# Two ways of loading q and k for the last eight attention units of a fused attention and two-MLP kernel

## The chip, the cores and the metric

The kernel runs as one program on one core of a Trainium2 chip. The metric is the device time of one execution in microseconds. Each kernel is run several times and the median stands for it. One further execution is run under the hardware profiler, and every row of a trace in this document is from such a profiled execution.

## The reference, cut to what matters

q, k and v are float32 arrays of 8 batches x 8 heads x 576 rows x 64 columns. Attention is computed within chunks of 64 rows only:

```
scores = (q_c @ k_c^T) / 8          # per batch, head and chunk of 64 rows
attn   = softmax(scores)            # minus the row's maximum, exp, divided by the row's sum
x      = attn @ v_c                 # laid out as 4608 tokens x 512
xn     = x / rms(x) * rms_g
x      = (silu(xn @ w_gate) * (xn @ w_val)) @ w_out          # 512 -> 1536 -> 512
out    = (h * relu6(h + 3) / 6) @ w_out2 ,  h = x @ w_in2    # 512 -> 2048 -> 512
```

## The kernel before

TensorE's time goes to the two MLPs. Their weights and activations are each split into a high and a low part, and three products of 128x128 by 128x512 (high x high, low x high, high x low) stand for one. The 4608 tokens are nine blocks of 512. The first three blocks run through the first MLP one by one (36 steps each), with the weights in SBUF. The other six run in three **passes** of two blocks, in which seven sums of operands replace eight products. Operands of the passes are read again from device memory, 512 KB at a time, by `Loads.ahead` (line 472 for the operands of the up products, `wo`, and line 478 for those of the down products, `wd`). Six such transfers are issued ahead, and each use of one issues another, so that a `wo` is asked for six operands before its use. An operand serves 12 products.

**The clock of the order.** The program's order is written out by hand in steps called ticks. `tick()` (line 1199) first emits what the agenda holds for this tick and then calls `some(n)` (line 1145), which takes n waiting transfers from a queue of attention loads and issues them on SP (SyncE's queue). n is 3 in the passes. A pass has 66 ticks: 42 of the up products, with 12 products (one operand) in each, and 24 of the down products, with 12 products in each. P0 is the first tick of the passes. All engines run their own instructions in this order, and SP issues its transfers in this order too.

**Attention** is worked in units of 256 tokens and is spread between the products. Units 4 to 9 (class `Pair`, line 737) run under the first three blocks, units 10 to 17 (class `Wide`, line 891, a subclass of `Pair`) under the first two passes, four to a pass, at ticks 0, 14, 28 and 42 of the pass. `STEPS_P` (line 43) lists their steps: turn_q at 0, turn_k at 1, then scores, maximum, subtraction, exp, sum, and so on until values at 13. `attend` (line 1162) runs a step. When it has run turn_k of a unit it hands q and k of the next unit to the queue (`give`), and when it has run values it hands over v. Before turn_q it calls `until`, which issues at once whatever of this unit's q and k is still in the queue.

- `Pair.parts_qk` (line 751) places heads so that 64 rows of SBUF hold one head's 64 columns after a turn. It reads runs of 32 columns (128 bytes): one transfer moves 32 rows x 8 runs, 32 KB, and a unit needs 16 transfers each for q and k (24 each where it crosses the end of a batch with 64 and 192 tokens, 32 each where it crosses with 128 and 128).
- `Wide.parts_qk` (line 894) reads eight rows of a head at once (2 KB) for two heads. One transfer moves 128 KB, and a unit needs 4 each for q and k (8 each where it crosses a batch).
- `turned` is a transpose of 32x32 blocks on VectorE. In `Pair` it reads and writes in plain order (line 780), in `Wide` with strides (line 908).
- `Pair.scores` (line 790) multiplies over 64 rows and makes all scores of the unit in 32 products of 64x64 by 64x64. `Wide.scores(e)` (line 913) multiplies over 32 rows and sums two such products, so that 32 products make half of the unit's scores, e = 0 or 1. It runs twice, at ticks 3 and 5 of the unit, with its own maximum (`top`, line 936) behind each. A float32 product shows as two instructions in the trace, so that 32 products are 64 instructions.

The buffers of q, k, their turned forms and v are single: the first transfer into q waits until the unit before has turned its q, and likewise for k. The passes also carry `Stash` (line 281), which prepares the second MLP's weights on VectorE, ScalarE and GpSimd and loads and stores them on ScalarE's own queue: 16 transfers in 24 ticks.

Of the kernel before, what the change touches and what calls it, by code (L numbers as in the profile page):

```python
# [10 lines left out]
F32 = mybir.dt.float32  # L11
# [3 lines left out]
ALU = mybir.AluOpType  # L15
AX = mybir.AxisListType


def _f32_of(word):
# [23 lines left out]
STEPS_P = (  # L43
    (0, ("turn_q",)),
    (1, ("turn_k",)),
    (3, ("scores0", "top0")),
    (5, ("scores1", "top1")),
    (6, ("less",)),
    (7, ("expo",)),
    (9, ("total", "share")),  # L50
# [24 lines left out]
def fused_kernel(  # L75
# [13 lines left out]
    nc = tc.nc  # L89
    B, H, S, D = q.shape  # L90
    NT, DM = out.shape
    CH = 64
# [6 lines left out]
    NP = H // 2  # L99
# [14 lines left out]
    sm_p = ctx.enter_context(tc.tile_pool(name="sm", bufs=4))  # L114
# [10 lines left out]
    PS = ps_p.tile([128, 8, 512], F32, name="PS")  # L125
    yd = [dr_p.tile([128, KD, N], F32, name=f"yd{b}") for b in range(NB)]
    ATT, GB, VB, YB = 0, 2, 3, 4
# [358 lines left out]
    def runs(t0, n):  # L486
        done = 0
        while done < n:
            b, s = divmod(t0 + done, S)
            step = min(n - done, S - s)  # L490
            yield done, step, b, s
            done += step
# [5 lines left out]
    def side(a, j):  # L498
        return j ^ a // 2

    class Att:
# [37 lines left out]
        def scores(self):  # L539
            self.s = PS[:, self.bank:self.bank + 2, 0:256]  # L540
            ps = self.s.rearrange("p z (e c k) -> p z e c k", e=2, c=2)
            qT = self.qT.rearrange("p (a t) -> p a t", a=NP)
            kT = self.kT.rearrange("p (a t) -> p a t", a=NP)
            for a, c, j in FOURS:
                x = side(a, j)
                nc.tensor.matmul(
                    ps[x * 64:(x + 1) * 64, a // 2, a % 2, c, :],
                    qT[j * 64:(j + 1) * 64, a, c * 64:(c + 1) * 64],
                    kT[j * 64:(j + 1) * 64, a, c * 64:(c + 1) * 64],
                    start=True,  # L550
                    stop=True,
                )

        def top(self):
            self.mx = sm_p.tile([128, 2, NP], F32, tag="mx", name="mx")
            s = self.s.rearrange("p z (x k) -> p z x k", k=CH)
            nc.vector.tensor_reduce(out=self.mx, in_=s, axis=AX.X, op=ALU.max)
# [111 lines left out]
        def run(self, *steps):  # L669
            for st in steps:  # L670
                getattr(self, st)()

    class Half(Att):
# [12 lines left out]
        def parts_qk(self):  # L686
            self.q, self.k = self.bufs("q", "k")
            for dst, src in ((self.q, q), (self.k, k)):
                d = dst.rearrange("p (h d) -> p h d", h=H)
                for off, n, b, s in runs(self.i * 128, 128):  # L690
                    nc.sync.dma_start(out=d[off:off + n], in_=src[b, :, s:s + n, :].rearrange("h p d -> p h d"))
                    yield
# [41 lines left out]
    TP = 256  # L734
    NPR = NT // TP

    class Pair:
# [38 lines left out]
                    nc.sync.dma_start(out=d[off:off + n], in_=v[b, :, s:s + n, :].rearrange("h p d -> p h d"))  # L776
                    yield

        def turned(self, to, x):
            nc.vector.transpose(out=to, in_=x)  # L780

        def turn_q(self):
            self.qT = self.buf("qT")
            self.turned(self.qT, self.q)

        def turn_k(self):
            self.kT = self.buf("kT")
            self.turned(self.kT, self.k)

        def scores(self):  # L790
            ps = PS[:, ATT:ATT + 2, :].rearrange("p z (t e c k) -> p z t e c k", t=2, e=2, c=2)
# [90 lines left out]
            nc.vector.tensor_tensor(ss, sq[:, 0:256], sq[:, 256:512], op=ALU.add)  # L882

        def run(self, st):
            if st[-1].isdigit():
                getattr(self, st[:-1])(int(st[-1]))
            else:
                getattr(self, st)()


    class Wide(Pair):


        def parts_qk(self):

            self.q, self.k = self.buf("q"), self.buf("k")
            for dst, src in ((self.q, q), (self.k, k)):
                d = dst.rearrange("p (h x) -> p h x", h=2)
                for off, n, b, s in runs(self.i * TP, TP):
                    for g in range(4):  # L900
                        h = g // 2 + 2 * (g % 2)
                        sv = src[b, h:h + 5:4, s:s + n, :].rearrange("h (t u) d -> t h (u d)", u=8)
                        r = g * 32 + off // 8
                        nc.sync.dma_start(out=d[r:r + n // 8], in_=sv)
                        yield

        def turned(self, to, x):
            nc.vector.transpose(
                out=to.rearrange("p (h g t u) -> p h u g t", h=2, g=2, u=8),
                in_=x.rearrange("p (h u g f) -> p h u g f", h=2, u=8, g=2),  # L910
            )

        def scores(self, e):
            ps = PS[:, ATT:ATT + 2, :].rearrange("p z (t e c k) -> p z t e c k", t=2, e=2, c=2)
            self.s = PS[:, ATT:ATT + 2, :].rearrange("p z (x k) -> p z x k", k=CH)
            qT, kT = (
                x.rearrange("p (h g n) -> p g h n", h=2, g=2) for x in (self.qT, self.kT)
            )
            for t in range(2):
                for y in range(2):  # L920
                    for g in range(2):
                        for h in range(2):
                            for j in range(2):
                                c = h ^ y
                                f = slice((2 * j + e) * 32, (2 * j + e + 1) * 32)
                                n = slice((2 * t + c) * 64, (2 * t + c + 1) * 64)
                                x = side(2 * h + e, j)
                                nc.tensor.matmul(
                                    ps[x * 64:(x + 1) * 64, h, t, e, c, :],
                                    qT[f, g, h, n],  # L930
                                    kT[f, g, h, n],
                                    start=g == 0,
                                    stop=g == 1,
                                )

        def top(self, e):
            if e == 0:
                self.mx = sm_p.tile([128, 2, 2 * NP], F32, tag="mx", name="mx")
            nc.vector.tensor_reduce(
                out=self.mx.rearrange("p z (t e c) -> p z t e c", t=2, e=2)[:, :, :, e],  # L940
                in_=self.s.rearrange("p z (t e c) k -> p z t e c k", t=2, e=2)[:, :, :, e],
                axis=AX.X,
                op=ALU.max,
            )

    XN = {}

# [168 lines left out]
    with tc.manual_schedule():  # L1116
# [20 lines left out]
                first[int(op[-1])].run(op[:-1])  # L1137
        xf.pop(0)

        unit = [(Pair if i < 10 else Wide)(i) for i in range(NPR)]  # L1140
        chain = [Half(i) for i in range(NTL, 2 * NTL)] + unit[4:]
        supply = deque()
        ready = set()
# [1 line left out]
        def some(n):  # L1145

            while n > 0 and supply:
                if next(supply[0][1], True):
                    ready.add(supply.popleft()[0])
                else:  # L1150
                    n -= 1
# [44 lines left out]
        P0 = 2 * HK  # L1196
        clock = [-HK]

        def tick():
            t = clock[0]  # L1200
            for _, fn in sorted(agenda.pop(t, ()), key=lambda x: x[0]):
                fn()
            some(8 if t < 0 else 5 if t < P0 - 14 else 3)
            clock[0] += 1

        for blk, due in (
# [118 lines left out]
        for b in range(3):  # L1325
            prev, late = None, None
            hk = 0
            for f in range(FA):
                mm_up(GB, whole(W["gate", f]), xs)
                s = sg_p.tile([128, N], F32, tag="sg", name="sg")  # L1330
# [33 lines left out]
        for p in range(3):  # L1364
            b = 3 + 2 * p
            bk = {0: (2, 3), 1: (6, 7), 4: (4, 5)} if p % 2 == 0 else {0: (6, 7), 1: (2, 3), 4: (4, 5)}
            g = {}
# [16 lines left out]
            for i in range(NI + 1):  # L1384
# [13 lines left out]
                for n, (pr, m) in enumerate(slots):  # L1398
                    i_ = i - 1 if pr in (3, 4) else i
                    k_, x, z = {  # L1400
                        1: (S00, B11, 0), 2: (S01, B21, 0), 3: (S4, B22, 4), 4: (S11, T4, 1),
                        5: (S1, T1, 4), 6: (S2, T2, 1), 7: (S3, T3, 1),
                    }[pr]
# [14 lines left out]
                    elif (pr, m) == (3, 0):  # L1418
                        t = gt(h0, 1)
                        vec(t, t, bank(4, 0), ALU.add)  # L1420
                        later = t
                    elif (pr, m) == (4, 1):
                        t = gt(h1, 0)
# [3 lines left out]
                    elif (pr, m) == (3, 1):  # L1427
                        s = hold.pop("s2")
                        vec(s, s, bank(4, 1), ALU.add)
                        t = gt(h0, 1)  # L1430
# [8 lines left out]
                    elif (pr, m) == (2, 1):  # L1439
                        t = gt(f0, 0)  # L1440
                        vec(t, t, bank(0, 1), ALU.mult)
                    elif (pr, m) == (7, 0):
                        t = gt(f1, 1)
# [3 lines left out]
                    elif (pr, m) == (7, 1):  # L1447
# [3 lines left out]
                        t = gt(f1, 1)  # L1451
                        nc.gpsimd.tensor_tensor(t, t, s3, op=ALU.mult)
                    if n % 2 == 1:
                        tick()
# [67 lines left out]
        for n, f in enumerate(fs):  # L1522
            bank = 6 + n % 2
            i, m, z = f // 4, f // 2 % 2, f % 2
# [5 lines left out]
            s = sg_p.tile([128, N], F32, tag="sg", name="sg")  # L1530
# [124 lines left out]
        for b in range(1, NB, 2):  # L1655
# [7 lines left out]
            for I in range(NG + 1):  # L1663
# [7 lines left out]
                for pr, m in slots:  # L1671
                    I_ = I - 1 if pr in (3, 4) else I
                    i = 2 * I_ + m
                    k_, x, z = {
                        1: (A11, B11, Z0), 2: (A12, B21, Z0), 3: (S4_, B22, Z4), 4: (A22, T4, Z1),
                        5: (S1_, T1, Z4), 6: (S2_, T2, Z1), 7: (S3_, T3, Z1),
                    }[pr]
# [14 lines left out]
                    elif pr == 3:  # L1692
                        t = slot(i, "12")
# [7 lines left out]
                    elif pr == 7:  # L1701
                        t = slot(i, "22")
# [37 lines left out]
            for n, (pr, i) in enumerate(steps):  # L1740
                k_, z = {
                    1: (O11, Z0), 2: (O12, Z0), 3: (O4, Z4), 4: (O22, Z1),
                    5: (O1, Z4), 6: (O2, Z1), 7: (O3, Z1),
                }[pr]
# [7 lines left out]
                if i == NQ - 1:  # L1752
# [5 lines left out]
                    elif pr == 7:  # L1758
                        c = keep("c22", Z1)
# [4 lines left out]
                    elif pr == 3:  # L1764
                        c = held.pop("u2")
# [15 lines left out]
        for m in range(2):  # L1781
            for i in range(NQ):
                for wi, xi in ((0, 0), (1, 0), (0, 1)):
# [4 lines left out]
                        start=False,  # L1788
                        stop=False,
# [37 lines left out]
```

## Time and profile before

| | us |
|---|---|
| median of 3 runs | 1682.11 (1678.25 to 1682.73) |
| the profiled execution, whole | 1679.51 |
| its span, first to last instruction | 1677.7 |

The profile's views show, for one execution, the share of each engine, groups of instructions by line of the kernel, who waited for whom, and instructions in order of time. PE is TensorE's products and PEld its weight loads, DVE is VectorE, ACT is ScalarE, POOL is GpSimd, SPq and ACTq are the queues on which SyncE and ScalarE issue transfers. Times of rows are us from the span's start. The passes begin at about 379 us.

### The profile page before, as it was taken

To read this page: it belongs to the slowest core of one execution; us is meant where nothing else is said; L and a number is where in the kernel's file an instruction comes from. 1 tells how busy PE (TensorE), PEld (TensorE's weight loads), DVE (VectorE), ACT (ScalarE), POOL (GpSimd) and SP (SyncE) were. 2 spreads that over 40 slices of the span, in tenths; PEclk is the share of its full clock that TensorE was granted. 3 is DMA by queue.
4 is the path that set the end of the run, shared out by engine and by line. 5 is a ranking of instruction groups with operands and counts; after the bars stand their busy time and mean duration, and the time that the engine had idled before them with its cause. 6 is when DMAs were issued, how large, how long until landed. Compare 5 with 4: busy or idle time off the path is not lost.

```text
span 1677.7 us, 26541 instructions
## 1 busy us (share of the span) xinstructions
PE 1649.2 (98%) x9920; PEld 1350.7 (81%) x9920; DVE 1086.8 (65%) x1600; ACT 845.2 (50%) x1409; POOL 459.5 (27%) x336
## 2 busy tenths in 40 slices
PE   8999999999999999999999999999999999999998
PEld 7777888878878888788887888888788878887886
DVE  6998566656575775758436378448746764874475
ACT  6786344455454454645434344455445544654552
POOL 1001434321326522364226622131023003301310
PEclk8999999999999999999999999999999999999999
DMA  9913777747876488855979766667767786777665
GB/s 301 271 37 71 207 208 222 205 152 251 292 262 224 168 297 286 290 176 185 361 238 316 293 239 226 213 190 250 219 209 224 209 243 191 223 218 235 189 200 150
DMA packets 336096, 375.07 MB, mean 224 GB/s; under 512 B 184288, under 2 KB 260064, under 8 KB 335840
## 3 DMA queue, kind: packets, MB, share of 16 engines
q1 hardware_dynamic: 273984, 302.84, 58.4%
q10 hardware_dynamic: 61984, 70.53, 12.2%
q8 instruction: 79, 1.29, 0.3%
q14 instruction: 49, 0.40, 0.1%
HBM read 292.55 MB, written 80.74 MB: 223 GB/s over the span
## 4 chain that ended last, share of the span: by engine, by line
PE 45%; DVE 5%; DMA 1%; ACT 1%; issue 1%; SPq 1%; DVEq 0%; POOL 0%; ACTq 0%; POOLq 0%
PE PS L1034 24%; PE PS L1584 13%; PE PS L1023 2%; DVE gs L1578 1%; PE PS L1051 1%; PE PS L1048 1%; PE PS L1049 1%; DVE gt L1720 1%; PE PS L1056 1%; PE PS L1057 1%; PE PS L1060 1%; SPq L1603 1%; DMA stash_in<-sc 1%; PE PS L1784 1%; DVE oq L1598 0%
## 5 line engine op out<-in xcount | busy, mean ns | idle before, releaser
L1034 PE MATMUL PS<-xu,wo 128*128 128x512 f32 x1512 | 353.1, 392 | 3.4 <-DVE gu L1362 2.3
L1034 PEld LDWEIGHTS PS<-xu,wo 128*128 128x128 f32 x1512 | 282.3, 188 | 65.0 <-DVE gu L1362 3.1
L1034 PE MATMUL PS<-xo,wq 128*128 128x512 f32 x1344 | 305.3, 389 | 0.0
L1584 PE MATMUL PS<-gs,wq 128*128 128x512 f32 x1296 | 296.2, 390 | 2.4 <-DVE gs L1578 2.0
L1034 PEld LDWEIGHTS PS<-xo,wq 128*128 128x128 f32 x1344 | 252.3, 188 | 52.4
L1584 PEld LDWEIGHTS PS<-gs,wq 128*128 128x128 f32 x1296 | 242.7, 188 | 55.3 <-DVE gs L1578 5.0
L1023 PE MATMUL PS<-XH,w 128*128 128x512 f32 x576 | 148.9, 401 | 5.1 <-ACT sg L1331 3.1
L1023 PEld LDWEIGHTS PS<-XH,w 128*128 128x128 f32 x576 | 108.0, 191 | 29.2 <-ACT sg L1331 3.8
L1048 PE MATMUL PS<-gs,wd 128*128 128x512 f32 x288 | 113.4, 394 | 1.6 <-DVE gu L1362 1.6
L1049 PE MATMUL PS<-gs,wd 128*128 128x512 f32 x288 | 112.2, 390 | 0.0
L1079 POOL TENSOR_TENSOR al<-sg,ah 128x512 fp32r<-128x512 f32 x40 | 56.2, 1404 | 156.2 <-ACT ah L1077 151.9
L1358 POOL TENSOR_TENSOR gs<-gu,gs 128x512 fp32r<-128x512 f32 x60 | 86.6, 1461 | 42.7 <-ACT gs L1357 33.9
L1651 POOL TENSOR_TENSOR gt<-gx 128x512 f32<-128x512 f32 x8 | 10.3, 1289 | 299.8 <-DVE gx L1648 299.8
L1362 DVE TENSOR_TENSOR gu<-gu,PS 128x512 f32<-128x512 f32 x60 | 41.0, 685 | 77.4 <-ACT gu L1444 42.0
L1578 DVE TENSOR_TENSOR gs<-gu,gs 128x512 fp32r<-128x512 f32 x88 | 67.9, 792 | 31.4 <-ACT gs L1577 31.1
L1577 ACT CAST gs<-gt 128x512 fp32r<-128x512 f32 x96 | 58.3, 623 | 49.6 <-DVE gt L1720 44.3
L1515 DVE SCALAR_TENSOR_TENSOR gu<-gu,PS 128x512 f32<-128x512 f32 x48 | 32.8, 684 | 72.6 <-ACT gu L1512 72.6
L1023 PE MATMUL PS<-XL,w 128*128 128x512 f32 x288 | 78.9, 396 | 0.0
L1077 ACT CAST ah<-sg 128x512 fp32r<-128x512 f32 x52 | 32.3, 621 | 88.9 <-DVE sg L1335 63.2
L1051 PE MATMUL PS<-gs,wd 128*128 128x512 f32 x288 | 77.0, 389 | 0.0
L1577 ACT CAST gs<-gu 128x512 fp32r<-128x512 f32 x96 | 57.2, 621 | 22.8 <-DVE gs L1578 15.6
L1651 POOL TENSOR_TENSOR gt<-gu 128x512 f32<-128x512 f32 x24 | 32.5, 1355 | 129.0 <-DVE gu L1648 124.9
(251 smaller groups left out, 2887.6 us busy)
## 6 DMA issues: line engine op xcount, KB each, us to landing
wq<-stash_in SPq DMA_DIRECT2D x128, 512.0 KB
wo<-ops SPq DMA_DIRECT2D x126, 512.0 KB
wq<-sums_out SPq DMA_DIRECT2D x64, 512.0 KB
wq<-stash_out SPq DMA_DIRECT2D x48, 512.0 KB
wd<-keep_out SPq DMA_DIRECT2D x36, 512.0 KB
yd<-yst SPq DMA_DIRECT2D x18, 512.0 KB
ops<-w ACTq DMA_DIRECT2D x36, 256.0 KB
v<-in_v_dram SPq DMA_DIRECT2D x32, 256.0 KB
```

What stands on the lines that cost most here:

```text
L1023: nc.tensor.matmul(ps, w(wi, c), xs[c][xi], start=(i == 0), stop=(i == n - 1))
L1034: nc.tensor.matmul(PS[:, bank, :], op[:, wi, c * 128:(c + 1) * 128], x[xi][:, c, :], start=first and i == 0, stop=last and i == 5, skip_gr ...
L1048: nc.tensor.matmul(ps, wm[0], a[0], start=first, stop=False)
L1049: nc.tensor.matmul(ps, wm[1], a[0], start=False, stop=False)
L1051: nc.tensor.matmul(PS[:, banks[m], :], w[:, 0, m * 128:(m + 1) * 128], a[1], start=False, stop=last)
L1079: nc.gpsimd.tensor_tensor(lo, t, hi.bitcast(F32), op=ALU.subtract)
L1358: nc.gpsimd.tensor_tensor(w[:, 1, :], t, w[:, 0, :].bitcast(F32), op=ALU.subtract)
L1362: nc.vector.tensor_tensor(o, x, y, op=op)
L1577: nc.scalar.copy(w[:, 0, :], x)
L1578: e.tensor_tensor(w[:, 1, :], x, w[:, 0, :].bitcast(F32), op=ALU.subtract)
L1584: nc.tensor.matmul(PS[:, banks[m], :], op[:, wi, m * 128:(m + 1) * 128], x[xi], start=first and (wi, xi) == (0, 0), stop=False, skip_group ...
L1651: nc.gpsimd.tensor_tensor(slot(i, "t"), slot(i, "12"), slot(i, "11"), op=ALU.subtract)
```

## The change

The class `Wide` goes, and all units are `Pair`. In the passes the scores are made in one step at tick 4 of the unit in place of two at ticks 3 and 5, and `some` issues four waiting transfers per tick in place of three.

```diff
 STEPS_P = (
     (0, ("turn_q",)),
     (1, ("turn_k",)),
-    (3, ("scores0", "top0")),
-    (5, ("scores1", "top1")),
+    (4, ("scores", "top")),
     (6, ("less",)),
...
-    class Wide(Pair):
-        def parts_qk(self):
-            self.q, self.k = self.buf("q"), self.buf("k")
-            for dst, src in ((self.q, q), (self.k, k)):
-                d = dst.rearrange("p (h x) -> p h x", h=2)
-                for off, n, b, s in runs(self.i * TP, TP):
-                    for g in range(4):
-                        h = g // 2 + 2 * (g % 2)
-                        sv = src[b, h:h + 5:4, s:s + n, :].rearrange("h (t u) d -> t h (u d)", u=8)
-                        r = g * 32 + off // 8
-                        nc.sync.dma_start(out=d[r:r + n // 8], in_=sv)
-                        yield
-        def turned(self, to, x):
-            nc.vector.transpose(
-                out=to.rearrange("p (h g t u) -> p h u g t", h=2, g=2, u=8),
-                in_=x.rearrange("p (h u g f) -> p h u g f", h=2, u=8, g=2),
-            )
-        def scores(self, e):
...
-        def top(self, e):
...
-        unit = [(Pair if i < 10 else Wide)(i) for i in range(NPR)]
+        unit = [Pair(i) for i in range(NPR)]
...
-            some(8 if t < 0 else 5 if t < P0 - 14 else 3)
+            some(8 if t < 0 else 5 if t < P0 - 14 else 4)
```

`turn_q` and `turn_k` call the plain transpose directly.

## Rows read from the trace of the kernel before

**Rows 1.** The page's first part: busy time, share of the span, instructions.
```profile
PE 1649.2 (98%) x9920; PEld 1350.7 (81%) x9920; DVE 1086.8 (65%) x1600; ACT 845.2 (50%) x1409; POOL 459.5 (27%) x336
```

**Rows 2.** Groups by line, TensorE: busy us, mean ns, idle before, releasers.
```profile
L1034 PE MATMUL PS<-xu,wo 128*128 128x512 f32 x1512 | 353.1, 392 | 3.4 <-DVE gu L1362 2.3 <-DVE s L1362 0.9 <-DVE xu L1248 0.2
L928 PE MATMUL PS<-kT,qT 32*64 32x64 f32 x1024 | 18.7, 221 | 0.9 <-DVE kT L908 0.9
```

**Rows 3.** Timeline of TensorE in unit 12: start, us, count, idle before.
```profile
478.81 4.42 PE L1034 MATMUL PS<-xu,wo 128*128 128x512 f32 x18
485.49 2.93 PE L1034 MATMUL PS<-xu,wo 128*128 128x512 f32 x6 [2.26 <-DVE gu L1362]
...
489.57 2.80 PE L1034 MATMUL PS<-xu,wo 128*128 128x512 f32 x11
```

**Rows 4.** Two stretches: engines' busy time, granted clock, DMA share, GB/s.
```profile
486.00:488.00 2.00, 2.00 (x6) 1.34 (x4) 2.00 (x3) 0.00 (x0) 1.66 (x1) 0.50 1.00 364
680.00:720.00 40.00, 39.11 (x350) 31.38 (x349) 32.02 (x42) 24.32 (x36) 15.27 (x11) 1.00 0.86 282
```

**Rows 5.** Waits of SP's queue, 378 to 715 us: total, times, longest.
```profile
SPq L904 <- DVE qT L908: 14.7, 4, 6.2
SPq L904 <- DMA wo<-ops: 14.7, 8, 3.3
```

**Rows 6.** Waits of ScalarE for transfers, first 150 to 378, then 378 to 715.
```profile
ACT sg L1331 <- DMA ops<-oh: 5.6, 1, 5.6
...
ACT xu L1245 <- DMA sraw<-in_moe_w_out_dram: 3.2, 1, 3.2
```

**Rows 7.** Timeline of TensorE around score steps of units 10 and 9.
```profile
391.36 5.73 PE L1034 MATMUL PS<-xu,wo 128*128 128x512 f32 x24
397.03 1.16 PE L928 MATMUL PS<-kT,qT 32*64 32x64 f32 x64
398.12 2.11 PE L1034 MATMUL PS<-xu,wo 128*128 128x512 f32 x8
...
335.71 1.16 PE L799 MATMUL PS<-kT,qT 64*64 64x64 f32 x64
336.81 0.50 PE L1048 MATMUL PS<-ah,w 128*128 128x512 f32 x1
```

**Rows 8.** Groups by line, VectorE: turns and maxima of both classes.
```profile
L908 DVE STREAM_TRANSPOSE qT<-q 128x1024 f32<-128x1024 f32 x8 | 17.4, 2175 | 0.0
L908 DVE STREAM_TRANSPOSE kT<-k 128x1024 f32<-128x1024 f32 x8 | 17.2, 2156 | 0.0
L939 DVE TENSOR_REDUCE mx<-PS 128x8 f32<-128x512 f32 x16 | 10.9, 684 | 22.5 <-PE PS L928 22.4
...
L780 DVE STREAM_TRANSPOSE qT<-q 128x1024 f32<-128x1024 f32 x6 | 7.4, 1238 | 0.0
L809 DVE TENSOR_REDUCE mx<-PS 128x16 f32<-128x1024 f32 x6 | 7.3, 1221 | 1.9 <-PE PS L799 1.9
L780 DVE STREAM_TRANSPOSE kT<-k 128x1024 f32<-128x1024 f32 x6 | 7.2, 1207 | 0.0
```

**Rows 9.** Timeline of SP's queue: loads of units 6 and 15, and `wo`.
```profile
189.55 8.87 SPq L768 DMA_DIRECT2D q<-in_q_dram  x16
198.46 3.88 SPq L764 DMA_DIRECT2D q<-in_q_dram  x8
...
591.65 1.15 SPq L904 DMA_DIRECT2D q<-in_q_dram  x3
...
614.35 6.21 SPq L472 DMA_DIRECT2D wo<-ops  x7
```

**Rows 10.** Timeline of TensorE: first use of the operand asked for at 614.35.
```profile
620.86 5.91 PE L1034 MATMUL PS<-xu,wo 128*128 128x512 f32 x24
```

**Rows 11.** SP's queue from 189.5 to 203.5, then 381 to 400: packets, MB, share.
```profile
q1 hardware_dynamic: 4320, 0.51, 23.5%
...
q1 hardware_dynamic: 1434, 4.31, 75.1%
```

More of the change, by code (lines that the diff above doesn't have):

```diff
@@ L777, in parts_v @@
                     yield
-        def turned(self, to, x):
-            nc.vector.transpose(out=to, in_=x)
         def turn_q(self):
             self.qT = self.buf("qT")
-            self.turned(self.qT, self.q)
+            nc.vector.transpose(out=self.qT, in_=self.q)
         def turn_k(self):
             self.kT = self.buf("kT")
-            self.turned(self.kT, self.k)
+            nc.vector.transpose(out=self.kT, in_=self.k)
         def scores(self):
@@ L884, in run @@
         def run(self, st):
[L885 to L888, printed above, removed]
-    class Wide(Pair):
-        def parts_qk(self):
-            self.q, self.k = self.buf("q"), self.buf("k")
-            for dst, src in ((self.q, q), (self.k, k)):
-                d = dst.rearrange("p (h x) -> p h x", h=2)
-                for off, n, b, s in runs(self.i * TP, TP):
-                    for g in range(4):
-                        h = g // 2 + 2 * (g % 2)
-                        sv = src[b, h:h + 5:4, s:s + n, :].rearrange("h (t u) d -> t h (u d)", u=8)
-                        r = g * 32 + off // 8
-                        nc.sync.dma_start(out=d[r:r + n // 8], in_=sv)
-                        yield
-        def turned(self, to, x):
-            nc.vector.transpose(
-                out=to.rearrange("p (h g t u) -> p h u g t", h=2, g=2, u=8),
-                in_=x.rearrange("p (h u g f) -> p h u g f", h=2, u=8, g=2),
-            )
-        def scores(self, e):
[L914 to L934, printed above, removed]
-        def top(self, e):
[L937 to L944, printed above, removed]
@@ L946, in fused_kernel @@
+            getattr(self, st)()
     XN = {}
```

## The prediction

> **What bounds the kernel now.** I read the page's shares first. TensorE is busy for 1649.2 us, 98% of the span [rows 1], so what counts is how long it takes for its own work and the few places where it waits. The groups by line show the places: in the passes the products of line 1034 waited 3.4 us in all and the score products 0.9 us, always for VectorE and never for a transfer [rows 2]. The timeline shows the largest of these waits: 2.26 us before 485.49 [rows 3]. The stretches show what came after it: the granted clock was 0.50 from 486 to 488 us, which is 1.2 GHz instead of 2.4, while at 680 to 720 us, with an idle of 0.9 us inside, it stayed at 1.00 [rows 4]. DMA is not the bound but is near it, with a share of 0.86 there. The waits of SP's queue show that it runs in order and is held often: q and k issues waited 14.7 us for the turn of the unit before and 14.7 us for landings of `wo`, which they do not read [rows 5]. From that I infer that only a limited number of transfers is in flight, in order, over all lines. ScalarE, which issues transfers from its own queue, also waited for landings: up to 5.6 us at once under the first three blocks, where q and k come in short runs, and up to 3.2 us in the passes [rows 6].
>
> **The change, part by part.** 1. *Scores.* One product of line 1034 takes 353.1 us / 1512 = 0.2335 us [rows 2]. Half a unit's scores on 32 rows take 1.09 us from their start to the next product (397.03 to 398.12), and the 24 products before them take 5.67 us where 24 x 0.2335 is 5.60, so a step costs 1.16 us of TensorE. A whole unit's scores on 64 rows take 1.10 us to the next product (335.71 to 336.81), the same 64 instructions [rows 7]. So the eight units lose eight steps: 8 x 1.16 = **9.3 us**, all of it on the bounding engine.
>
> 2. *Turns and maxima.* VectorE's two turns fall from 2175 + 2156 to 1238 + 1207 ns, and the maximum from 2 x 684 to 1221 ns [rows 8]: 1.9 + 0.15 us per unit, 16 us in all. VectorE is not the bound, so this counts only where TensorE waits for it. The scores also come one tick later after turn_k. So the 0.9 us of waits for kT [rows 2] should go. What is late next is the unit's maximum, which has two ticks until the subtraction.
>
> 3. *The stall at 485.* From 478.81 to 489.57 TensorE did 24 products and one score step, 24 x 0.2335 + 1.16 = 6.8 us of work, in 10.8 us: 4.0 us lost [rows 3], of which 2.26 is idle and the rest is the half clock [rows 4]. The product there waits for VectorE, which stood behind two turns (1.9 us shorter now) and a half maximum of 0.68 us (now one tick later). TensorE comes only 0.7 us earlier. I take the idle to shrink to about 0.4 us, a size that left the clock alone at 680 to 720 us, so 3.5 us come back. Bounds: 0 to 4.0. Sum of parts 1 to 3: 9.3 + 0.9 + 3.5 = **13.7 us**.
>
> 4. *More transfers on SP.* From the code, q and k of the eight units take 320 transfers after and 88 before. Units 11 and 15 need 48, unit 13 needs 64, the others 32. With four per tick the 13 ticks between turn_k and the next turn_q issue 52, so unit 13 has 12 left, which are issued at once in front of its turn_q. SP's own issue time hides beside TensorE; what can surface is lateness of what stands behind. Short runs were issued at 8.87 / 16 = 0.55 and 3.88 / 8 = 0.49 us each under the first blocks, where nothing else was on the queue. In the passes SP took from 591.65 to 614.35, 22.7 us, for 16 q and k issues and 4 `wo` [rows 9]: 1.1 us each, most of it waiting. The next `wo`, issued at 614.35, was used at 620.86 [rows 10], a lead of 6.5 us, and TensorE did not wait for it. An operand is asked for six operands ahead, which is 6 x 12 x 0.2335 = 17 us, so some 10 us of lead can be lost without a wait. Each operand now has four q or k issues and one `wo` in its tick, five issues in the 12 x 0.2335 = 2.8 us for which TensorE uses it. So the pace decides: at up to 0.56 us per issue SP keeps up, at 0.8 us it loses 5 x 0.8 - 2.8 = 1.2 us per tick, or 14 us over the 12 ticks of a long unit, against those 10 us. I take 0.65 us, nearer to the row of the same transfers (0.49 to 0.55) than to 1.1, because the waits behind the 1.1 were for 512 KB landings, and with four small transfers to each large one fewer of these are in flight. That loses 0.45 us per tick, 5 us per long unit, within the lead. No operand is then late. I price the rest by ScalarE: one wait of up to 5.6 us [rows 6] in each of the three long units, of which TensorE sees about 1.5 us, or **4.5 us given back**. Bounds: 0, and 30 us if the pace were 0.9 us at all three. Unit 13's k lands late by at most 12 x 0.55 = 7 us, but its turn lies at the start of the down products, where TensorE does not wait for VectorE at every product, and its scores come three ticks later; it is in the 4.5 us.
>
> The engines' own time is a smaller matter. In short runs SP's queue moved 0.51 MB in 23.5% of 14 us, 6.5 us per MB, and with 512 KB transfers 4.31 MB in 75.1% of 19 us, 3.3 us per MB [rows 11]. A unit's q and k are 1 MB, so the passes gain about 3 us of transfer time per unit, 26 us on some 400, which lifts a share of 0.86 to about 0.92. The Trainium skill speaks against this part: "DMA: Bandwidth & Descriptors", section "Bandwidth", says that transfers under 64 KB are dominated by their descriptors; the doubled price per MB agrees, and by the fixed 2.0 us per transfer that the same page fits for GpSimd's path (section "Anatomy of one DMA"), taken one behind the other, 232 more transfers would be 464 us of queue time, an estimate that the issue rows contradict, since 24 transfers went out in under 13 us.
>
> **Sum.** 13.7 - 4.5 = 9.2 us. The profiled execution took 1679.5 us, 2.6 below the median of the runs shown; it would become 1670.3, and the median about **1673**.
>
> **The rivals.** *A, nothing given back (chance 0.09):* the queue hides everything. For it: under the first blocks the same loads cost TensorE nothing visible. Against it: nothing there had to arrive on time. 13.7 us off, 1668.4.
>
> *B, given back whole (0.27):* the pace is 0.8 us. Each long unit overruns its lead by 14 - 10 = 4 us, three times 12 to 13 us, and the time is 1681, no change. For it: the 1.1 us of the passes. Against: the mix is of smaller transfers.
>
> *C, slower (0.23):* operands come late. At 0.85 us per issue a long unit loses (4.25 - 2.8) x 12 = 17 us, 7 more than its lead, three times 22 us; net 22 - 13.7 = 8 slower, 1690. It decides from 0.8 us per issue on, at the `wo` issues behind the loads of units 11, 13 and 15; for it is the lead of 6.5 us even now, and that each wait of this length can halve the clock for a while as at 485; against it, that TensorE never waited for a `wo` so far.
>
> *D, the step does not halve (0.03):* the scores on 64 rows cost two steps' time in the passes. The rows of units 9 and 10 are alike, so almost nothing is for it. It leaves 13.7 - 9.3 - 4.5, no change.
>
> **How the numbers follow.** My forecast has 0.38. A measurement of this kernel can tell about 0.3%, 5 us, from no change. Faster: 0.38 + 0.09 = 0.47. Within: 0.27 + 0.03 = 0.30. Slower: 0.23. The likeliest case's own range is 1668 to 1677, by 0 to 4 us in part 3 and 1 to 8 in part 4. The range for all cases goes from 1667, everything of parts 1 to 3 at its best and nothing given back, to 1691, just past C's value; cases beyond either end keep under 0.2.
>
> **What would show it.** Right: score steps of 64x64 products, eight in the passes, each 1.1 us; turns of 1.24 us; no idle of over 1 us near unit 12's fourth tick and the clock at 1.00 there; q and k issues on SP at 0.5 to 0.7 us, `wo` leads not under 4 us, and TensorE's waits still for VectorE or ScalarE. Wrong: products of line 1034 that wait for `wo`; ScalarE held by landings for over 5 us several times with TensorE idle behind it; new stretches of half clock in the passes; a turn of k on VectorE that waits for its load in the up products.

## The result, and the profile after

The changed kernel takes **1704.63 us** (1701.44 to 1705.76, 4 runs) against 1680.18 for the kernel before in the same comparison: ratio 1.0142, 95% interval [1.0119, 1.0165], some 24 us slower. The prediction was 1673, with a range up to 1691. It had the sign wrong and the result lies outside its range. Ratios below are turned into microseconds as (ratio - 1) x 1680, so that kernels timed on different chips can be set side by side.

The page's first part and the groups by line answer to [rows 1], [rows 2] and [rows 8]:

```profile
PE 1649.3 (97%) x9408; PEld 1347.2 (79%) x9408; DVE 1069.3 (63%) x1592; ACT 843.9 (50%) x1409; POOL 458.8 (27%) x336
```
```profile
L972 PE MATMUL PS<-xu,wo 128*128 128x512 f32 x1512 | 355.3, 394 | 15.1 <-DMA wo<-ops 8.6 <-ACT s L1387 1.8 <-ACT gu L1371 1.6
L986 PE MATMUL PS<-gs,wd 128*128 128x512 f32 x288 | 115.7, 402 | 13.2 <-ACT gs L1295 8.7 <-DVE yst L1026 1.7 <-DVE gu L1300 1.6
...
L780 DVE STREAM_TRANSPOSE qT<-q 128x1024 f32<-128x1024 f32 x14 | 17.3, 1236 | 0.0
L784 DVE STREAM_TRANSPOSE kT<-k 128x1024 f32<-128x1024 f32 x14 | 17.1, 1220 | 10.9 <-DMA v<-in_v_dram 8.4 <-DMA k<-in_k_dram 2.6
```

512 score instructions are gone (9920 to 9408), the turns take 1.2 us, and yet TensorE is as busy as before, because some of its products ran slower. It also stood still more: span less busy time is 53.5 us instead of 28.5. The products for `wo` waited 15.1 us instead of 3.4, mostly for the transfer itself, and the down products waited 13.2 us (1.6 before), mostly for ScalarE's cast at line 1295.

Nearly all of it lies in the passes. The last wait of 1.6 us for VectorE in the third pass stands in both traces at the same work. Timeline of TensorE, start and length of a group of products, first the kernel before, then the changed one:

```profile
904.42 0.50 PE L1048 MATMUL PS<-gs,wd 128*128 128x512 f32 x1 [1.61 <-DVE gu L1362]
```
```profile
928.06 0.50 PE L986 MATMUL PS<-gs,wd 128*128 128x512 f32 x1 [1.61 <-DVE gu L1300]
```

That is 23.6 us later, while the wait just ahead of the passes stands at 376.41 and 376.29. The two spans differ by 25.1 us in all. The first two passes in stretches (busy time of TensorE, weight loads, VectorE, ScalarE, GpSimd, then granted clock, DMA share, GB/s), the middle one for the kernel before and all three for the changed one:

```profile
505.00:565.00 60.00, 60.00 (x507) 49.30 (x506) 33.16 (x40) 30.30 (x47) 37.28 (x27) 1.00 0.66 213
```
```profile
378.00:505.00 127.00, 124.16 (x844) 100.32 (x843) 79.25 (x112) 66.58 (x101) 30.86 (x22) 1.00 0.82 246
505.00:565.00 60.00, 47.09 (x307) 35.94 (x306) 23.89 (x27) 20.99 (x34) 29.70 (x22) 0.92 0.78 222
565.00:720.00 155.00, 144.91 (x977) 117.22 (x976) 94.29 (x130) 75.05 (x115) 46.90 (x32) 0.98 0.77 231
524.00:532.00 8.00, 4.45 (x12) 3.47 (x12) 1.44 (x2) 1.69 (x3) 2.52 (x2) 0.57 0.68 176
688.00:695.00 7.00, 5.81 (x73) 4.47 (x74) 1.98 (x3) 0.88 (x1) 0.00 (x0) 0.52 1.01 390
```

Between 505 and 565 us, the down products of the first pass, TensorE was never idle before and now stands for 12.9 us. It is there that the last of unit 13's 64 transfers, those of its k, come in. The last two rows lie around the two longest stalls: the granted clock is 0.57 and 0.52 there, near the lower of its two levels (1.2 instead of 2.4 GHz), as it was after the stall at 485 us in [rows 4].

What the engines waited for, 378 to 715 us (total us, times, longest), TensorE, then ScalarE, VectorE and SP's queue:

```profile
PE PS L986 <- ACT gs L1295: 8.7, 3, 5.1
PE PS L972 <- DMA wo<-ops: 8.6, 4, 4.2
...
ACT gu L1291 <- DMA q<-in_q_dram: 12.7, 3, 5.0
ACT gs L1295 <- DMA k<-in_k_dram: 10.8, 2, 6.9
...
DVE kT L784 <- DMA v<-in_v_dram: 8.4, 1, 8.4
...
SPq L767 <- DMA wo<-ops: 34.0, 26, 4.0
```

ScalarE's casts read neither q nor k, so these are waits of the transfers that ScalarE itself issues just ahead of them. The 8.4 us of VectorE are those of unit 13's k: the row names v, but the turn at 530.56 us reads k, the last of whose transfers SP issued at 526.55 and which landed at 530.19. How this runs is seen around the largest stall. Timelines of TensorE, ScalarE and SP's queue:

```profile
521.40 1.07 PE L989 MATMUL PS<-gs,wd 128*128 128x512 f32 x4
527.55 0.79 PE L986 MATMUL PS<-gs,wd 128*128 128x512 f32 x1 [5.08 <-ACT gs L1295]
```
```profile
519.29 0.67 ACT L276 CAST shi<-sraw 128x512 fp32r<-128x512 f32 x1
526.44 0.40 ACTq L247 DMA_DIRECT2D sraw<-in_moe_w_out_dram  x1
526.88 0.62 ACT L1295 CAST gs<-gu 128x512 fp32r<-128x512 f32 x1 [6.92 <-DMA k<-in_k_dram]
```
```profile
502.59 6.33 SPq L767 DMA_DIRECT2D k<-in_k_dram  x7
509.02 0.85 SPq L477 DMA_DIRECT2D wd<-keep_out  x2
509.92 6.68 SPq L767 DMA_DIRECT2D k<-in_k_dram  x8
516.69 0.89 SPq L477 DMA_DIRECT2D wd<-keep_out  x2
517.63 1.94 SPq L767 DMA_DIRECT2D k<-in_k_dram  x4
519.73 0.34 SPq L477 DMA_DIRECT2D wd<-keep_out  x1
520.12 6.86 SPq L767 DMA_DIRECT2D k<-in_k_dram  x12
```

ScalarE is done at 519.96 and then holds its next issue, a load for `Stash`, until 526.44; the cast that TensorE needs stands behind it. In the trace's records each transfer of SP and ScalarE raises one of eight semaphores (numbers 100, 102, 104, 105 and 107 to 110), which the two queues take in turn in the order of the program, and an issue waits until the transfer that had the semaphore before has landed. The load at 526.44 takes number 110, which a k transfer had that SP issued only at 524.65. So ScalarE waits until the transfer eight places before its own in the program's order has been issued by SP and has landed: it waits until SP has caught up. SP was behind: 36 issues from 502.59 to 527.08, 0.68 us each. SP's own issues wait for these eight semaphores too, as its 34.0 us of waits for `wo` before q and k show.

### The profile page after: what moved, and what is told of

Read it like the earlier page. It is cut to its first block, busy times and chain, and to the rows that moved or that the text cites. A ratio compares the mean times of both kernels' runs of the same rounds, so it can differ in the third digit from the quotient of the medians.

```text
span 1702.8 us, 25739 instructions
## 1 busy us (share of the span) xinstructions
PE 1649.3 (97%) x9408; PEld 1347.2 (79%) x9408; DVE 1069.3 (63%) x1592; ACT 843.9 (50%) x1409; POOL 458.8 (27%) x336
## 4 chain that ended last, share of the span: by engine, by line
PE 51%; DVE 6%; DMA 6%; SPq 2%; issue 1%; ACT 1%; ACTq 0%; DVEq 0%; POOL 0%; POOLq 0%
PE PS L972 25%; PE PS L1522 13%; PE PS L986 3%; DMA wo<-ops 3%; PE PS L989 3%; PE PS L987 3%; PE PS L961 2%; DVE gs L1516 2%; SPq L767 1%; DVE gt L1658 1%; DMA q<-in_q_dram 1%; PE PS L994 1%; PE PS L995 1%; PE PS L998 1%; PE PS L1722 1%
## 5 line engine op out<-in xcount | busy, mean ns | idle before, releaser
L972 PE MATMUL PS<-xu,wo 128*128 128x512 f32 x1512 | 355.3, 394 | 15.1 <-DMA wo<-ops 8.6
L986 PE MATMUL PS<-gs,wd 128*128 128x512 f32 x288 | 115.7, 402 | 13.2 <-ACT gs L1295 8.7
L987 PE MATMUL PS<-gs,wd 128*128 128x512 f32 x288 | 113.5, 394 | 0.0
L989 PE MATMUL PS<-gs,wd 128*128 128x512 f32 x288 | 78.1, 393 | 0.0
L986 PEld LDWEIGHTS PS<-gs,wd 128*128 128x128 f32 x288 | 54.9, 191 | 28.6 <-ACT gs L1295 10.4
```

The source lines that it names most:

```text
L972: nc.tensor.matmul(PS[:, bank, :], op[:, wi, c * 128:(c + 1) * 128], x[xi][:, c, :], start=first and i == 0, stop=last and i == 5, skip_gr ...
L986: nc.tensor.matmul(ps, wm[0], a[0], start=first, stop=False)
L987: nc.tensor.matmul(ps, wm[1], a[0], start=False, stop=False)
L989: nc.tensor.matmul(PS[:, banks[m], :], w[:, 0, m * 128:(m + 1) * 128], a[1], start=False, stop=last)
```

## The experiments

**Transfers, their number and their length.** Three kernels make the compute of the changed kernel and fill the same tiles, but from other places of q and k, so that number and length of runs can be set apart: 88 transfers with 4 KB runs, 88 with 128-byte runs, 320 with 1 KB runs (the long runs are shorter in units 11, 13 and 15, which cross a batch). At the same bytes more transfers are also smaller ones, 16 to 32 KB instead of 64 to 128; these two the runs cannot part. The changed kernel itself is the fourth corner, 320 with 128-byte runs.

```diff
-        unit = [Pair(i) for i in range(NPR)]
+        unit = [(Pair if i < 10 else Other)(i) for i in range(NPR)]
...
+                    pieces = 1
...
+                                k0 = (j * 2 + g) * 512 + o * 16
+                                sv = rows[k0:k0 + 16 * x].rearrange("(t x) f -> t (x f)", t=32)
+                                nc.sync.dma_start(out=to, in_=sv)
```

> The changed kernel, but q and k of the last eight units come in 88 transfers (as before) of 4 KB runs, as many bytes, from places that are not the right ones (so scores and output are other numbers; all other work is unchanged). Theory N (the number of transfers costs: each of the 320 takes a place among the few that may be in flight, so that wo, wd and ScalarE's own transfers queue behind small ones): the whole loss goes and the gain of the scores shows, 1666 to 1671 us. Theory R (the 128-byte runs cost: they take the transfer engines twice the time per byte): the same, 1666 to 1671. Neither N nor R, but the single score step or the new order of the steps: still about 1700.

> As few_long, with 88 transfers, but every byte of q and k of the last eight units in runs of 128 bytes, as in the changed kernel (again other numbers). Theory N: 1667 to 1675 us, the short runs alone cost a few us at most. Theory R: 1698 to 1706, as the changed kernel.

> 320 transfers as in the changed kernel, 32 KB each, but in runs of 1 KB (again other numbers). Theory N: 1698 to 1706 us, as the changed kernel, with TensorE waiting for wo and for ScalarE's casts in the same places. Theory R: 1667 to 1675.

| transfers | long runs | 128-byte runs |
|---|---|---|
| 88 | 1671.11, ratio 0.9944 [0.9926, 0.9961], -9.4 us | 1673.79, 0.9964 [0.9951, 0.9977], -6.0 us |
| 320 | 1693.29, 1.0079 [1.0063, 1.0094], +13.3 us | 1704.63, 1.0142 [1.0119, 1.0165], +23.9 us |

The number of transfers costs 22.7 us with long runs and 29.9 with short ones. The length of the runs costs 3.4 us at 88 transfers, where the two intervals overlap, and 10.6 at 320. The third kernel, with many long runs, came out faster than theory N had it (1698 to 1706), since the short runs' share was missing. So the number is the cause, and the short runs add to it mostly where there are many of them. Wherever the loads are few, the change wins; the 13.7 us of parts 1 to 3 did not come whole. In the run with 88 long transfers the wait at 485 us is down to 0.7 us and another has come up at unit 15 (waits of TensorE, 378 to 720 us):

```profile
PE PS L993 <- DVE ge L1321: 2.5, 1, 2.5
PE PS L993 <- DVE s L1321: 1.5, 1, 1.5
PE PS L993 <- DVE gu L1321: 0.7, 1, 0.7
```

**Four per tick in the kernel before.**

```diff
-            some(8 if t < 0 else 5 if t < P0 - 14 else 3)
+            some(8 if t < 0 else 5 if t < P0 - 14 else 4)
```

> The kernel before with four waiting transfers per tick in place of three, nothing else. Theories N and R: 1680 us as before, within 3 us, since 88 large transfers are done either way in six ticks or less. Theory P (the pace of four per tick crowds out the operands): slower by 5 us or more.

1679.06, ratio 0.9991 [0.9979, 1.0003]. Asking for more per tick is nothing by itself when there are few to ask for.

**Which units.** The new loading for some units only; the others stay `Wide`. First for units 10, 12, 14, 16 and 17 (32 transfers each, four per tick), then for 10 and 14 with three per tick.

```diff
+        unit = [(Pair if i < 10 or i in (10, 12, 14, 16, 17) else Wide)(i) for i in range(NPR)]
```

> Short runs only for units 10, 12, 14, 16 and 17, which lie in one batch (32 transfers each); units 11, 13 and 15, which cross a batch (48, 64, 48), are loaded and scored as before. Four per tick as in the change. Theory L (the long units, unit 13's 64 transfers above all, hold ScalarE and wo; 32 fit between): 1670 to 1677 us, no cast of the down products of the first pass waits over 2 us. Theory E (every unit pays by its transfers, 31 us over 232 extra): 120 extra transfers cost 16 us, against 5 steps of 1.16 us saved: 1690 us.

> Short runs only for units 10 (loaded before the passes begin) and 14 (loaded during the down products, 23 ticks ahead), the others as before, three per tick as before. If short runs cost nothing where neither wo nor ScalarE's transfers are close: two score steps less, 1676 to 1679 us, 2 to 4 below before. Theory E: 48 extra transfers, 6 us, 1684.

1681.1, ratio 1.0003 [0.9992, 1.0015], and 1679.8, 1.0001 [0.9992, 1.001]. The steps saved, 5.8 and 2.3 us, were used up in both, and both times lie between their two theories. By what they were used up is not shown here; the pace is tried again below.

**ScalarE's issues moved.** The changed kernel with the transfers of `Stash` issued on SP.

```diff
-            nc.scalar.dma_start(out=o, in_=w_src(self.kind, self.f))
+            nc.sync.dma_start(out=o, in_=w_src(self.kind, self.f))
```

> The changed kernel with the transfers of the second MLP's weights (Stash) issued on SP in place of ScalarE, all else equal. Theory A (ScalarE, held at its own issues until a place is free, keeps casts of the down products waiting): ScalarE's waits for landings go from the passes, the idle of about 17 us between 505 and 562 goes to under 4, and the time falls by 8 to 15 us to 1690 to 1697, unless SP now holds wo behind GpSimd. Theory W (late wo is what matters): 1700 to 1715, since SP has still more to issue in order.

1692.18, ratio 1.0075 [1.0053, 1.0097]: 11.3 us come back, as theory A had it. Its other forecast failed: between 505 and 565 us TensorE still stands for 9.8 us, where the changed kernel had 12.9 (the 17 of the expectation is too high), and ScalarE still waits 11.3, 10.2 and 7.7 us, now where it reads loads of `Stash`, which stand on SP. What is left stands open in its trace (waits of TensorE, then of VectorE, 378 to 820 us):

```profile
PE PS L972 <- DMA wo<-ops: 9.8, 5, 5.0
PE PS L795 <- DVE kT L784: 7.7, 1, 7.7
...
DVE kT L784 <- DMA k<-in_k_dram: 14.8, 1, 14.8
```

Unit 13's k is 14.8 us late for VectorE, and the scores wait 7.7 us for it. With ScalarE's issues out of the way this wait is seen by itself.

**q and k on GpSimd's queue.** The changed kernel with these loads issued by GpSimd.

> The changed kernel with q and k of the last eight units issued on GpSimd's queue, 320 transfers of 128-byte runs as before, so that SP's order of wo and ScalarE's issues have nothing in front of them. Theory N (places in flight and order shared with SP and ScalarE): TensorE no longer waits for wo and the casts are on time, 1670 to 1680 us. If GpSimd pays over 0.7 us for each issue, its products of the passes come late instead: 1690 to 1720, with waits for GpSimd's lines in their place.

1785.98, ratio 1.0637 [1.0617, 1.0657], beyond both expectations. This is a test of another cost rather than of the queue: GpSimd also computes in the passes, and TensorE waited for those products, first of all for the scaled p (28.7 us) and for gs (20.5 us). One issue took about 0.55 us of GpSimd's own time, eight in 4.37 us:

```profile
537.32 4.37 POOL L902 DMA_DIRECT2D k<-in_k_dram  x8
```

Its products no longer waited for `wo` in the passes, but it cannot tell what the wait between SP and ScalarE is worth, and the run stays out of the sum.

**Scores one tick later in the kernel before.** Only the first half's tick is changed.

```diff
-    (3, ("scores0", "top0")),
+    (4, ("scores0", "top0")),
```

> The kernel before with one number changed: the first half of the scores of the last eight units one tick later, directly ahead of the second half. Transfers are those of before. If the stall at 485 us comes from scores that are asked for too soon after the turn of k, it goes, with the 0.9 us of waits for kT: 1675 to 1677. Rival: the wait only moves to another product, as it did in the run with 88 long transfers (2.9 us at 617 us): 1679 to 1680, no change.

1684.51, ratio 1.0026 [1.0015, 1.0037], slower than either theory had it. The wait at 485 us stays (1.8 us) and a new one comes, the second half's scores behind the first half's maximum. (The wait at 617 us that the expectation cites is 2.5 us in its trace, not 2.9.) So the later tick alone does not relieve 485 us; what is left is the shorter turns and the single step, which no run parts. Waits of TensorE, 378 to 720 us:

```profile
PE PS L928 <- DVE mx L939: 4.0, 1, 4.0
PE PS L1034 <- DVE gu L1362: 1.8, 1, 1.8
```

**Unit 13 alone, operands earlier, middle units slower.** Three edits: in the kernel before, unit 13 alone in the new way (at four per tick, which by itself changed nothing above); in the changed kernel, ten operands ahead instead of six; and the five middle units with three per tick and eight ahead.

```diff
+        unit = [(Pair if i < 10 or i in (13,) else Wide)(i) for i in range(NPR)]
...
-                at((66 if p == 0 else P0 + p * PAIR - 8) + t, loads.ahead, 1)
+                at((66 if p == 0 else P0 + p * PAIR - 8) + t, loads.ahead, 2 if p == 0 and t < 4 else 1)
```

> The kernel before, in which unit 13 alone has its q and k in 64 transfers of 128-byte runs and its scores in one step; 48 more transfers than unit 13 had. Theory L (the loss sits in the units whose loads leave no slack, and unit 13 is the worst): 9 to 15 us slower than before, 1689 to 1695, with the waits between 505 and 562 us as in the changed kernel. Rival E (each transfer costs its share, 31 us / 232 = 0.13 us): 48 x 0.13 = 6.4 us less one step of 1.2 us, 1684 to 1686.

> The changed kernel with the operands wo and wd asked for ten instead of six ahead: in the first four ticks of the down products' loads two are asked for, so that every later one has four more operands' time to land. Theory that late operands share in the loss: the waits of products for wo (8.6 us in the changed kernel) go, and 5 to 9 us with them, 1696 to 1700. Theory that only ScalarE's blocked issues matter: no change, 1704.

> The five units between the long ones (10, 12, 14, 16 and 17) in 128-byte runs with scores in one step, the others as before, as in the run where this gave 1681, but with three transfers asked for per tick instead of four, and operands eight ahead instead of six. Five steps of 1.16 us are saved. Theory that crowding at four per tick ate them: 1673 to 1677. Rival: the 120 added transfers cost what the steps save wherever they are asked for: 1679 to 1682.

Unit 13 alone: 1685.68, 1.004 [1.0024, 1.0055], +6.7 us, as the rival's even share had it. Ten ahead: 1700.54, 1.0119 [1.0105, 1.0133], 3.9 us less than the changed kernel, below the 5 to 9 us expected and not clear of noise, since the intervals overlap. Products no longer wait for `wo` at all in its trace; about half of what they had waited came back as other waits (378 to 820 us: for VectorE 7.4 us instead of 4.5, for ScalarE 14.3 instead of 13.2). Middle units, slower: **1672.73**, 0.9953 [0.9941, 0.9966], and in its trace no product waits for a transfer in the passes.

**Cures together.** The kernel before with `Stash` on SP; the changed kernel with `Stash` on SP and ten ahead; the same with unit 13 kept `Wide`; the five middle units, slower, with `Stash` on SP.

> The kernel before with the three stash transfers issued on SP instead of ScalarE, nothing else. Theory (ScalarE is held at its issues only because 232 transfers were added): nothing to win, 1677 to 1682. Rival (ScalarE's issues cost the kernel before as much): about 12 us faster, 1668.

> The changed kernel with both cures: stash transfers issued on SP, and operands asked for ten ahead. With the stash on SP alone it took 1692, and there its trace still has two waits for wo (3.3 and 5.4 us) and one of 8 us for unit 13's k. Theory (three separate carriers): the two wo waits go, 1682 to 1686. Rival (the cures take away the same waits): 1690 to 1693.

> As the run with both cures, but unit 13 alone keeps its loads in long runs and its scores in two steps: 184 transfers more than before, less 48, and seven of the eight steps saved (8.1 us). Theory (ScalarE, late wo and unit 13's k are all there is): 1671 to 1676. Rival (a cost per transfer that none of the three names, 0.05 us or more each): 1682 or more.

> The run with five units in short runs, three transfers per tick and operands eight ahead (1672.7), with the stash transfers on SP as well. Its trace shows no wait of a product for a transfer in the passes. Theory: nothing is left to win, 1671 to 1675. Rival: ScalarE's issues still hold something, 1666 to 1670.

The kernel before gains nothing from the move: 1678.49, 0.9995 [0.9986, 1.0004], so the 11.3 us belong to the added transfers. Both cures: 1693.33, 1.0079 [1.0063, 1.0095], no better than the move alone: the theory of separate carriers fell. The waits for `wo` are gone, 6.3 us for VectorE at line 1300 have come, and the scores of unit 13 still wait 8.4 us for its k. With unit 13 kept `Wide`: 1678.39, 1.0004 [0.9995, 1.0013], between the two expectations; against 1.0079 this is 12.6 us. The stretch of unit 13 is whole again, and one long stall is left, at 671 us, where ScalarE and VectorE wait for a load of `Stash` that now stands behind the q and k on SP. Stretch 505 to 565 us, then the timelines of ScalarE, VectorE and TensorE of this kernel:

```profile
505.00:565.00 60.00, 60.00 (x503) 49.38 (x503) 36.76 (x41) 28.16 (x45) 35.91 (x27) 1.00 0.71 210
```
```profile
669.09 0.66 ACT L266 ACTIVATE sc<-sraw 128x512 f32<-128x512 f32 x1 [11.82 <-DMA stash_in<-slo]
```
```profile
669.79 0.43 DVE L267 TENSOR_SCALAR sc<-sc 128x512 f32<-128x512 f32 x1 [13.59 <-ACT sc L266]
```
```profile
671.32 8.41 PE L1045 MATMUL PS<-xu,wo 128*128 128x512 f32 x24 [6.16 <-DVE gu L1373]
```

SP's lateness had not gone. It had only been handed from ScalarE's issue to ScalarE's operand.

The five middle units with `Stash` on SP: **1669.12**, 0.9943 [0.9931, 0.9955], the fastest of all. Its interval overlaps that of the same kernel without the move, so what the move adds there is not settled. Its products for `wo` wait 2.2 us in all:

```profile
L1045 PE MATMUL PS<-xu,wo 128*128 128x512 f32 x1512 | 350.0, 391 | 2.2 <-DVE s L1373 1.4 <-DVE gu L1373 0.8
```

**Unit 13 kept `Wide` and nothing else; the middle units with the old lead.**

> The changed kernel with unit 13 alone in long runs and two score steps; ScalarE's issues and the operands' lead as in the changed kernel. With both cures unit 13 was worth 15 us. Theory (unit 13's 64 transfers between 505 and 562 us are half the loss, whatever else is there): 1686 to 1692. Rival (without the cures the other units' waits eat it): 1698 or more.

> The run with five middle units in short runs and three transfers per tick (1672.7), with operands six ahead as before instead of eight. Theory (the pace made the gain): 1671 to 1676. Rival (the lead made it): 1679 to 1682, as with four per tick.

Without unit 13: 1687.84, 1.005 [1.0031, 1.007], 15.5 us less than the changed kernel. Of them 1.2 us are lost again by the step that unit 13 does not save, so its loads cost 16.7 us. Middle units, three per tick, old lead: 1674.87, 0.997 [0.996, 0.9981]. Compared with four per tick (1.0003) the pace made 5.5 us; the longer lead some 3 more, with intervals that overlap.

## Why the prediction was wrong

*Part 1, the scores: right.* The score instructions of the eight units went from 18.7 us of busy time [rows 2] to 16.3 x 512 / 896 = 9.3 us:

```profile
L795 PE MATMUL PS<-kT,qT 64*64 64x64 f32 x896 | 16.3, 221 | 0.0
```

*Parts 2 and 3, the turns and the stall at 485: right at their place.* The turns took 1236 and 1220 ns, and the score products waited for nothing (0.0 in the row above, 0.9 before). At the stall's place the changed kernel waited 0.72 us at a clock of 1.00:

```profile
483.57 8.69 PE L972 MATMUL PS<-xu,wo 128*128 128x512 f32 x37 [0.72 <-DVE gu L1300]
```

The gain was real where the loads allowed it: five steps (5.8 us) and this stall (3.5 us by the prediction; the wait there is 0.76 us in that kernel's trace) make 9.3 us, and the five middle units with `Stash` on SP gained 9.6. With all eight units in few transfers part of it was lost to a new wait at unit 15.

*Part 4, more transfers: wrong, and this step alone turned the sign.* It gave back 4.5 us; the number of transfers and their short runs took 9.4 + 23.9 = 33.3. Its inference that few transfers are in flight, in order, over all lines was right: the trace shows eight semaphores for both queues. Its pace, 0.65 us, was right for unit 13 (0.68) and too low for units 11, 12, 15 and 16 (0.74, 0.75, 0.77 and 0.80, from a unit's first issue to its last with the operands between). What was made of the pace failed in three places.

First, **unit 13**. The step let its k be late by "at most 12 x 0.55 = 7 us" and hid it in the 4.5. It counted only the 12 transfers that were left after the ticks, as if SP kept up within them, though the same paragraph had SP falling behind by 5 us per long unit. The whole count at the measured pace is 64 loads and 13 operands at 0.68 us, 52.4 us, against 13 ticks of 2.8 us, 36.4: 16 us late by this estimate. VectorE's wait for this k was 14.8 us in the run that moved ScalarE's issues, and 8.4 in the changed kernel, where VectorE itself came later. Unit 13's loads were worth 16.7 us in the changed kernel, half of the loss, though only 6.7 + 1.2 = 7.9 us when they were added alone: the lateness of the neighbours falls on the same queue.

Second, **ScalarE**. The step priced "one wait of up to 5.6 us in each of the three long units", a wait for one landing as in [rows 6]. In the passes ScalarE's issue waits until SP has reached its place in the program's order, eight transfers back, and that transfer has landed, so it waits as long as SP is behind: 12.7 and 10.8 us in the two largest rows of such waits. TensorE waited 8.7 us for the casts of line 1295 alone. Moving these issues gave back 11.3 us.

Third, **the lead of the operands**. "No operand is then late" was wrong: `wo` was waited for 8.6 us. By the step's own rule a pace of 0.77 us loses 5 x 0.77 - 2.8 = 1.05 us per tick, 13 us over 12 ticks, more than the 10 us of lead. The step also looked for this at the long units only: 7.7 of the 8.6 us came behind the loads of unit 16, which has 32 transfers but follows directly on unit 15. Timelines of SP's queue and TensorE:

```profile
674.70 9.26 SPq L767 DMA_DIRECT2D k<-in_k_dram  x8
684.05 2.48 SPq L471 DMA_DIRECT2D wo<-ops  x5
```
```profile
689.19 2.93 PE L972 MATMUL PS<-xu,wo 128*128 128x512 f32 x6 [4.23 <-DMA wo<-ops]
```

But this was the smallest of the three: a longer lead gave back 3.9 us, with intervals that overlap, and nothing once ScalarE's issues were moved.

The parts do not add up one by one (unit 13 and ScalarE's issues together with the lead gave 23.2 us where they gave 15.5, 11.3 and 3.9 singly), and the account that fits the traces is that one lateness, that of SP's queue, comes out at whichever engine waits first. Of the 33.3 us, 10.1 remain after these cures. 1.2 of them are the step that unit 13 does not save. The stall at 671 us, the same lateness at ScalarE's operand, costs some 9 by its row (6.16 idle, then 24 products in 8.41 us where 5.6 is their time). With the 3.4 us that the short runs cost at 88 transfers this is already more than 10.1, so what each of them holds of the rest is open.

Of the rivals, C had the sign. Its condition, a pace from 0.8 us on, was met at unit 16 alone (0.80), and the queue was late enough at 0.68. Its mechanism, `wo` late behind units 11, 13 and 15, was the third in size, and no product waited for `wo` behind units 11 and 13. That its 1690 came nearest is therefore luck in good part.

## What to carry to other kernels

Count a queue's issues against the time until the last of them is needed, all of them together (loads and operands, and what is already behind), and do it for the tightest unit rather than for the mean: here one unit of 64 loads was half the loss in the changed kernel. Where an engine that computes also issues transfers, and its landings are tracked together with another queue's, price its wait as that queue's lateness and not as one landing. Taking the new form only where the queue has slack, at a slower pace, kept what those units had to gain: 1669 to 1675 us where the change everywhere gave 1705.

## What was not expected of the hardware

At the same bytes and the same number of transfers, runs of 128 bytes cost only 3.4 us more than runs of 4 KB on the whole kernel, hardly clear of noise, with 335616 packets on SP's queue instead of 272896. What cost was the number of transfers: those of up to 32 KB with 1 KB runs lost 22.7 us against those of up to 128 KB, at 284032 packets. The Trainium skill says that transfers under 64 KB are dominated by their descriptors ("DMA: Bandwidth & Descriptors", section "Bandwidth"). The loss of the small transfers agrees with that bound, but the packet counts do not make the number of pieces in a transfer its cause.

A stall of 4 to 5 us cost more than itself, as the one at 485 us in the kernel before had: after the one that ended at 527.55 us, with a granted clock of 0.57 from 524 to 532, the products took 0.63 us each until 531 us, where they took 0.40 us two microseconds later, as the timeline of TensorE shows:

```profile
528.14 0.63 PE L987 MATMUL PS<-gs,wd 128*128 128x512 f32 x1
...
533.68 0.40 PE L987 MATMUL PS<-gs,wd 128*128 128x512 f32 x1
```
